# The last pair's stores spread over three queues, later sums of value weights, and a newly planned order, in a linear-attention and gated-unit kernel

## The chip, the cores and the metric

The kernel runs on one core of a Trainium2 chip. Unless said otherwise, times inside an execution are counted from the start of its profiled span, which is about 1.8 us shorter than the device time of the same run. TensorE is "PE" in the profile, its weight loads "PEld", VectorE "DVE", ScalarE "ACT", GpSimd "POOL", SyncE "SP"; a "q" behind a name means that engine's sequencer.

## The reference, cut to what matters

```python
# q, k, v: (8 batches, 8 heads, 576 tokens, 64); everything in float32
kv  = einsum('bhsd,bhse->bhde', k, v)
out = einsum('bhsd,bhde->bhse', q, kv)
x   = out / sqrt(mean(out*out, -1) + 1e-6) * g_norm      # -> (8, 576, 512)
gate = sigmoid(causal convolution of x with 5 taps per channel)
result = ((x @ w_val) * gate) @ w_out                    # w_val, w_out: 512 x 512
```

The two weights reach the kernel as 64-bit floats. They are narrowed to 32 bits on the chip, in eight steps for each quarter of a weight: five on VectorE and three on ScalarE.

## The kernel before

One function holds a small scheduler. Every piece of work is a step with an engine, a planned duration, a wanted start and needs. The scheduler turns the steps into one order per engine, and that order is fixed in the program. A table of shifts, found by a search, moves the wanted starts. Four parts:

```python
    def keep_warm(n):                       # filler: products with the identity
        if n > 0:
            new_kv(0)
        for _ in range(n):
            nc.tensor.matmul(..., ident[:], ident[:], start=True, stop=True)
    ...
    def store(i, c):                        # four rows of blocks, one DMA each
        ot = st["ot", i, c]
        for j in range(HB):
            ...
            nc.sync.dma_start(
                out=rows_out[2 * i + bb, n], in_=ot[j * TB:(j + 1) * TB, :])
    ...
    for n in range(4):                      # sums of value weights, on VectorE
        plan.add(
            "DVE", 0.61, begin + 20.0 + n, val_sums, n, ...
        )
    ...
        idle_from = 9.0
        for start, step in plan.order():
            if step["engine"] == "PE" and start < 60.0:
                keep_warm(int((start - idle_from) / 0.3))
                idle_from = start + step["time"]
            step["fn"](*step["args"])
```

Wherever the plan has TensorE idle in the first 60 us, the program puts one identity product per 0.3 us of planned idleness, which stops the engine from standing still. Each such product shows as two records in the trace.

The batches are worked in pairs. The output of the last pair ends with three groups of four stores each: "block 6", "block 7" and the "single" block of what is left over of both batches.

## Time and profile before

| | before |
|---|---|
| time, median of 3 runs | 337.14 us (337.06 to 337.18) |
| profiled span, granted clock (of another run, of 338.08 us) | 336.3 us, 0.998 |
| first value product starts (timeline of TensorE) | 42.54 us |
| last product ends (timeline of TensorE) | 330.44 us |
| last store issued, last store landed (DMA landings) | 333.25 us, 334.95 us |

The views that carry this are in the prediction below. The chain of waits is read from top to bottom as start, length and who held things up. In the table by stretches each engine has its busy time with the number of instructions behind it.

### The profile page before, as it was taken

The numbers are of one execution on the slowest core, as the hardware profiler recorded it, in microseconds if no ns is written. First come the engines' busy times: TensorE is split into PE (matmuls) and PEld (weight loads), VectorE is DVE, ScalarE is ACT, GpSimd is POOL, SyncE is SP. The second block draws the span as 40 slices with busy tenths as digits, with TensorE's granted clock in tenths as the row PEclk, the third lists the DMA queues.
The fourth block names the chain that finished last, engine by engine and source line by source line (L and its number), as shares of the span: only waits on it lengthen the run. The fifth ranks groups of instructions, "written<-read, shape, count | busy, mean of one in ns | idle before, by whom it ended". The sixth has DMA issues, their size and how long they took to land.

```text
span 336.3 us, 6403 instructions
## 1 busy us (share of the span) xinstructions
PE 319.1 (95%) x2251; PEld 256.2 (76%) x2251; DVE 281.8 (84%) x504; ACT 151.7 (45%) x325; POOL 140.4 (42%) x178
## 2 busy tenths in 40 slices
PE   2978999999999999999999999999999999999992
PEld 2978878888888878857878877688888577888761
DVE  4535979999999999999788799999989999989601
ACT  5357686585234464352445325343446143534220
POOL 3004603733677438926604478532962193000000
PEclk9999999999999999999999999999999999999999
DMA  6999995699699597577944699622520035220232
GB/s 199 268 305 357 283 248 178 160 251 294 188 232 236 123 259 212 138 209 188 302 111 132 166 258 244 156 55 67 133 63 0 17 87 117 57 55 16 62 95 64
DMA packets 46014, 55.38 MB, mean 165 GB/s; under 512 B 15754, under 2 KB 36254, under 8 KB 45982
## 3 DMA queue, kind: packets, MB, share of 16 engines
q1 hardware_dynamic: 42750, 48.67, 53.9%
q0 software_dynamic: 3072, 6.30, 8.1%
q8 instruction: 18, 0.29, 0.4%
q14 instruction: 14, 0.11, 0.1%
q10 hardware_dynamic: 160, 0.00, 0.0%
HBM read 39.21 MB, written 9.44 MB: 145 GB/s over the span
## 4 chain that ended last, share of the span: by engine, by line
PE 85%; DVE 5%; SPq 4%; DMA 2%; issue 1%; ACT 1%; DVEq 0%; ACTq 0%
PE val L582 19%; PE a L720 14%; PE cb L720 12%; PE raw L484 10%; PE va L632 9%; PE kv L407 6%; PE vc L632 4%; PE out L663 4%; PE vb L632 2%; DMA k<-in_k_dram 2%; PE xTps L530 2%; SPq L267 2%; DVE gate L570 2%; PE qTps L445 1%; SPq L290 1%
## 5 line engine op out<-in xcount | busy, mean ns | idle before, releaser
L512 POOL TENSOR_TENSOR rt<-ss,mhalf 128x8 f32<-128x8 f32 (+1 forms) x40 | 71.0, 1785 | 100.4 <-DVE ss L506 100.3
L570 DVE SCALAR_TENSOR_TENSOR gate<-xT,cwT,gate 128x576 f32<-128x576 f32 x128 | 98.8, 810 | 1.6 <-ACT gate L564 1.3
L553 POOL DMA_DIRECT2D xT<-y x96 | 52.8, 557 | 35.9 <-PE a L720 14.3
L582 PE MATMUL val<-xT,wval 128*128 128x288 f32 x256 | 65.7, 408 | 0.0
L582 PEld LDWEIGHTS val<-xT,wval 128*128 128x128 f32 x256 | 47.6, 190 | 12.9 <-ACT xT L537 0.8
L484 PEld LDWEIGHTS raw<-kvbd,qT 128*128 128x128 f32 (+1 forms) x320 | 35.4, 180 | 6.0 <-issue 2.6
L484 PE MATMUL raw<-kvbd,qT 128*128 128x128 f32 (+1 forms) x320 | 38.9, 280 | 0.8 <-DVE x L520 0.8
L498 ACT ACTIVATE sq<-raw 128x512 f32<-128x512 f32 (+1 forms) x40 | 22.1, 553 | 26.6 <-PE raw L484 26.5
L720 PE MATMUL a<-wsum,sums 128*128 128x256 f32 x128 | 33.5, 384 | 0.6 <-ACT ot L731 0.6
L506 DVE TENSOR_REDUCE ss<-sq 128x8 f32<-128x520 f32 (+1 forms) x40 | 25.3, 633 | 9.7 <-ACT sq L498 9.5
L577 ACT ACTIVATE gate<-gate 128x576 f32<-128x576 f32 x32 | 21.7, 684 | 12.5 <-DVE gate L570 12.3
L720 PEld LDWEIGHTS a<-wsum,sums 128*128 128x128 f32 x128 | 23.7, 190 | 4.7 <-ACT ot L731 1.0
L595 DVE TENSOR_TENSOR gv<-gv,gate 128x576 f32<-128x576 f32 x32 | 23.6, 750 | 2.8 <-ACT gate L577 1.6
L591 ACT COPY gv<-val 128x288 f32<-128x288 f32 x32 | 12.7, 396 | 28.9 <-PE val L582 28.7
L520 DVE TENSOR_TENSOR x<-raw,rt 128x512 f32<-128x512 f32 (+1 forms) x40 | 24.7, 622 | 0.3 <-PE xTps L530 0.3
L729 DVE TENSOR_TENSOR ot<-cb,ot 128x256 f32<-128x256 f32 x32 | 13.4, 420 | 13.7 <-ACT ot L733 9.5
L564 ACT ACTIVATE gate<-xT,cwT 128x576 f32<-128x576 f32 x32 | 23.6, 773 | 1.0 <-DVE gv L595 0.8
L407 PEld LDWEIGHTS kv<-v,k 128*64 128x64 f32 x512 | 17.6, 137 | 6.7 <-issue 5.5
L407 PE MATMUL kv<-v,k 128*64 128x64 f32 x512 | 20.7, 226 | 1.8 <-DMA k<-in_k_dram 1.8
L632 PE MATMUL va<-xs,vsum 128*128 128x288 f32 x64 | 18.1, 406 | 0.0
L720 PE MATMUL cb<-wout,sums 128*128 128x256 f32 x64 | 17.2, 390 | 0.6 <-DVE ot L729 0.2
L720 PE MATMUL cb<-wsum,sums 128*128 128x256 f32 x64 | 16.7, 384 | 0.3 <-DVE sums L696 0.3
(106 smaller groups left out, 510.1 us busy)
## 6 DMA issues: line engine op xcount, KB each, us to landing
q<-in_q_dram SPq DMA_DIRECT2D x96, 140.0 KB, 3.9
out_dram<-ot SPq DMA_DIRECT2D x144, 64.0 KB, 1.7
v<-in_v_dram SPq DMA_DIRECT2D x16, 512.0 KB, 7.3
k<-in_k_dram SPq DMA_DIRECT2D x16, 512.0 KB, 7.5
xT<-y POOLq DMA_DIRECT2D x96, 64.0 KB, 3.6
w_wval<-in_moe_w_val_dram SPq DMA_DIRECT2D x4, 512.0 KB, 6.2
q<-in_q_dram SPq DMA_DIRECT2D x4, 512.0 KB, 8.2
w_wout<-in_moe_w_out_dram SPq DMA_DIRECT2D x4, 512.0 KB, 6.4
```

Source lines behind the costliest of these rows:

```text
L407: nc.tensor.matmul(kvp[r * D:(r + 1) * D, hp, :], st["k", b, half][:, h, j, :] if j < NJ else kl[:, 2 * hp + r, :], st["v", b, half][:, h, ...
L484: nc.tensor.matmul(raw[row * m:(row + 1) * m, col * P:(col + 1) * P], st["qT", b][:, hp, c * P:c * P + m], kv_bd[b % 2][:, hp, :], start=T ...
L506: nc.vector.reduce_sum(out=ss[:, 0:n], in_=st["sq", b, c][:, 0:n], axis=AX.X)
L512: nc.gpsimd.tensor_tensor(out=rt[:, 0:n], in0=st["ss", b, c][:, 0:n], in1=mhalf[:, 0:n], op=ALU.pow)
L520: nc.vector.tensor_tensor(out=x[:, 0:n * D].rearrange("p (h e) -> p h e", h=n), in0=st["raw", b, c][:, 0:n * D].rearrange("p (h e) -> p h ...
L553: nc.gpsimd.dma_start(out=xTs[b % 2][i * TB:(i + 1) * TB, :, first:first + P], in_=y[a * TB:(a + 1) * TB, i])
L564: nc.scalar.activation(out=gate[:], in_=xTs[b % 2][:, jt, HALO:SX], func=AF.Copy, scale=cwT[:, K - 1, jt:jt + 1])
L570: nc.vector.scalar_tensor_tensor(out=gate[:], in0=xTs[b % 2][:, jt, tap * TB:tap * TB + S], scalar=cwT[:, tap, jt:jt + 1], in1=gate[:], op ...
L582: nc.tensor.matmul(val[:], wval[:, kc, jt * P:(jt + 1) * P], xTs[b % 2][:, kc, HALO + n * SV:HALO + (n + 1) * SV], start=(kc == 0), stop=( ...
L595: nc.vector.tensor_tensor(out=both, in0=both, in1=st["gate", b, jt][:], op=ALU.mult)
L632: nc.tensor.matmul(st[bank, "val", b, mj][:], weights_[:, k], tokens()[:, k], start=(n in (0, 1, 3) and k == 0), stop=(k == NK // 2 - 1), ...
L720: nc.tensor.matmul(st[bank, i, p], tokens()[:, k], weights_[:, k], start=(n < 2 and k == 0), stop=(k == NK // 2 - 1), skip_group_check=True)
```

## The change

Intent: GpSimd and ScalarE take some of the last pair's stores, so that fewer issues stand one behind the other on SyncE. The sums of value weights (four VectorE operations) are wanted at 150 us of the plan; so far they were wanted soon after the first batch and ran at 40.2 to 42.8 us. Planned durations are corrected to measured ones, and the order is searched anew, so the whole table of shifts is different. The diff, cut to its core:

```diff
 SHIFTS = {
     ... (every entry is different)
-    def store(i, c):
+    def store(i, c, cols=slice(0, C), queues=(nc.sync,)):
         ot = st["ot", i, c]
         for j in range(HB):
             ...
-            nc.sync.dma_start(
-                out=rows_out[2 * i + bb, n], in_=ot[j * TB:(j + 1) * TB, :])
+            queues[j % len(queues)].dma_start(
+                out=rows_out[2 * i + bb, n, :, cols], in_=ot[j * TB:(j + 1) * TB, cols])
...
-                "PE", 0.87 * part, t, raw_product, b, c,
+                "PE", 0.905 * (1.0 if c < NJ else 0.62), t, raw_product, b, c,
...  (four more durations: 1.75 -> 1.82, 1.93 -> 1.95, 3.45 -> 3.6, 0.885 -> 0.9)
+                if b == B - 1 and m:
+                    last_stores(chunk, r, t + 6.8)
+                    continue
...
+    def last_stores(chunk, r, want):
+        kept = lambda n: ("kept", (chunk[0], 3, n))
+        if r == 0:                                   # block 6
+            plan.add("POOL", 2.4, want, store, *chunk, slice(0, C), (nc.gpsimd,), ...)
+            return
+        plan.add("SP", 2.0, want, store, *chunk, HIGH, (nc.sync,), ...)       # block 7
+        plan.add("SP", 1.0, want + 1.0, store, *chunk, LOW, (nc.sync, nc.scalar), ...)
...
-            "DVE", 0.61, begin + 20.0 + n, val_sums, n,
+            "DVE", 0.61, 150.0 + n, val_sums, n,
```

More of the change, by code (lines that the diff above doesn't have):

```diff
@@ L21 @@
 SHIFTS = {
-    "fast_product": {0: -31.5, 1: 1.5, 2: -4},
-    "gate_tap": {0: 13, 1: 77, 2: 43, 3: 77, 4: 87, 5: 70.5, 6: 69.5, 7: 67.5},
-    "keep_x": {0: -25},
-    "kv_product": {5: -4.5, 6: -4.5, 7: -10.5},
-    "load_half": {("k", 0): 7.5, ("k", 1): 13.5, ("k", 3): 6.5, ("k", 4): -7, ("k", 5): 34.5,
-        ("k", 6): 3.5, ("v", 0): -60.5, ("v", 1): 19.5, ("v", 2): 27.5, ("v", 4): 13, ("v", 5): -9.5,
-        ("v", 6): 3, ("v", 7): 9.5},
-    "load_q": {4: -11.5, 5: -12, 6: -14.5, 7: -11.5},
@@ L30 @@
-    "load_tails": {4: 4.5, 5: -101.5, 6: -108.5},
-    "narrow_weight": {("wout", 0): 36, ("wout", 1): 20.5, ("wout", 3): -39},
-    "normalise": {7: 10.5},
-    "out_product": {1: 38.5, 3: -6},
-    "raw_product": {4: -84, 5: -23, 6: -17.5},
-    "square": {2: -9},
-    "stage_weight": {("cw", 0): -235.5, ("wout", 0): 13, ("wout", 1): 22, ("wout", 3): -4,
-        ("wval", 2): -117, ("wval", 3): -123.5},
-    "store": {0: 57.5},
-    "sums": {2: 9.5, 5: -91},
-    "token_sums": {0: 11.5},
-    "turn_blocks": {6: 23, 7: 9},
@@ L42 @@
-    "turn_q": {2: 5.5, 3: 27.5},
-    "turn_x": {1: 3, 3: 7.5},
-    "val_fast": {7: 12.5},
-    "val_product": {0: 33.5, 1: 23, 3: 8.5},
-    "weight_sums": {0: 35.5},
-    "x_sums": {6: -9},
+    "fast_keep": {0: -30, 2: -143.5, 3: -149},
+    "fast_product": {0: -8, 1: 3, 2: 4, 3: -10.5},
+    "gate_start": {1: 5, 7: 29.5},
+    "gate_tap": {1: 42, 2: 73.5, 3: 65, 4: 50.5, 5: 49, 6: 85.5, 7: 69},
+    "gated": {0: 12},
+    "halo": {3: -38.5},
+    "keep_x": {1: 45.5},
+    "kv_product": {2: 28.5, 5: 51.5, 6: 5},
@@ new lines @@
+    "load_half": {("k", 1): 9.5, ("k", 3): -4.5, ("k", 4): -4.5, ("k", 5): 2.5, ("k", 6): -22.5,
+        ("v", 1): 4.5, ("v", 2): -3, ("v", 3): -5, ("v", 4): -5, ("v", 5): -12.5, ("v", 6): -12,
+        ("v", 7): 6.5},
+    "load_q": {7: -19.5},
+    "load_tails": {0: 3.5, 3: -1.5, 4: -19, 5: -19, 6: 16, 7: 7},
+    "narrow_weight": {("wout", 3): -7},
+    "normalise": {2: 15, 6: -146, 7: -9.5},
+    "out_product": {1: -4},
+    "raw_product": {3: -10, 4: -5.5, 5: -15.5, 6: -8.5, 7: 15},
+    "stage_weight": {("cw", 0): -103.5, ("wout", 0): -23, ("wout", 1): 57.5, ("wout", 2): 42.5,
+        ("wval", 1): -83.5, ("wval", 2): -103.5, ("wval", 3): -102.5},
@@ L48 @@
+    "sums": {3: 14.5},
+    "token_sums": {0: -128.5, 2: -20},
+    "turn_x": {7: -9},
+    "val_fast": {7: 2},
+    "val_keep": {5: -41},
+    "val_product": {0: 42.5, 1: 43.5, 2: 2},
+    "x_sums": {5: 14.5, 6: 16.5},
 }
@@ L822, in attention @@
             plan.add(
-                "POOL", 1.75 * part, t + 2.3, powers, b, c, needs=[("ss", key)], gives=[("rt", key)],
+                "POOL", 1.82 * part, t + 2.3, powers, b, c, needs=[("ss", key)], gives=[("rt", key)],
                 takes=[("rt", key)], frees=[("ss", key)],
@@ L853, in attention @@
                     gives=[("xT", b, a), ("moved", b, n)], frees=[("y", b)] if a == 0 else [],
-                    load=0.26 / RATE,
+                    load=0.32 / RATE,
                 )
@@ L937, in products @@
                 plan.add(
-                    "PE", 1.93, t, val_product, b, jt, n,
+                    "PE", 1.95, t, val_product, b, jt, n,
                     needs=[("xT", b, c) for c in HALVES[n]] + [("wval", jt)] + [("val", k) for k in made],
@@ L962, in single @@
         plan.add(
-            "PE", 3.45, first, out_product, *key,
+            "PE", 3.6, first, out_product, *key,
             needs=gated_all(b - 1, b) + [("wout", jt) for jt in range(NK)],
@@ L994, in outputs @@
                 plan.add(
-                    "PE", 0.885, t + 0.88 * n, fast_product, *key,
+                    "PE", 0.9, t + 0.88 * n, fast_product, *key,
                     needs=used + ([("fast", last)] if last else [])
@@ L1023, in outputs @@
             single(b, first + 12.4)
+    def last_stores(chunk, r, want):
+        kept = lambda n: ("kept", (chunk[0], 3, n))
+        if r == 0:
+            plan.add(
+                "POOL", 2.4, want, store, *chunk, slice(0, C), (nc.gpsimd,), needs=[kept(3), kept(5)],
+                frees=[("ot", chunk)], load=0.26 / RATE,
+            )
+            return
+        plan.add(
+            "SP", 2.0, want, store, *chunk, HIGH, (nc.sync,), needs=[kept(4)], frees=[("ot", chunk)],
+            load=0.13 / RATE,
+        )
+        plan.add(
+            "SP", 1.0, want + 1.0, store, *chunk, LOW, (nc.sync, nc.scalar), needs=[kept(6)],
+            frees=[("ot", chunk)], load=0.13 / RATE,
+        )
     def loads_kv(b, want):
```

## The prediction

> **What bounds the kernel now.** I read the page first (busy shares and the 40 slices), then the busy time by stretches, then the waits of TensorE, then the chain that ended last at its two ends, and last the instructions in order of time around the end.
>
> ```profile
> span 336.3 us, 6403 instructions
> PE 319.1 (95%) x2251; PEld 256.2 (76%) x2251; DVE 281.8 (84%) x504; ACT 151.7 (45%) x325; POOL 140.4 (42%) x178
> ...
> PE   2978999999999999999999999999999999999992
> ...
> DVE  4535979999999999999788799999989999989601
> ```
> TensorE is busy nearly without a break from the fifth slice to the last but one, and VectorE is close behind it. The losses that the page shows lie at the two ends. The next view sums busy time by stretch (length; PE; weight loads; VectorE; ScalarE; GpSimd; clock, DMA share, GB/s).
>
> ```profile
> 0.00:22.80 22.80, 14.80 (x149) 14.05 (x149) 9.20 (x35) 12.18 (x27) 2.68 (x10) 1.00 0.98 254
> 22.80:42.60 19.80, 18.86 (x281) 16.57 (x281) 16.05 (x29) 12.67 (x31) 9.64 (x9) 1.00 1.07 316
> ...
> 330.50:336.30 5.80, 0.00 (x0) 0.00 (x0) 0.00 (x0) 0.35 (x1) 0.00 (x0) 0.89 0.35 90
> ```
> For 22.8 us the DMA engines are full (0.98) and TensorE does little of use: much of its 14.8 us is warm-up products with the identity. The last 5.8 us are stores and shutdown alone. Between them TensorE's waits are small:
>
> ```profile
> PE raw L484 <- DVE x L520: 0.8, 1, 0.8
> PE a L720 <- ACT ot L731: 0.6, 1, 0.6
> PE cb L720 <- DVE sums L696: 0.3, 1, 0.3
> PE cb L720 <- DVE ot L729: 0.2, 1, 0.2
> ```
> That is 1.9 us between 44 and 331 us. More is lost in gaps too short to be called waits: after 42.6 us the useful work at the chain's back-to-back durations is 112 output products x 0.865, 32 value products x 1.94, 56 fast value products x 0.97, 4 single products x 3.58, about 28.8 of raw, 17.0 of kv and 3.5 of transposes, together 276.9 us. It took 330.4 - 42.6 = 287.8, so about 11 us go to hand-overs and waits. The chain at the start:
>
> ```profile
> 10.80 1.55 SPq L267
> ...
> 12.40 1.42 SPq L267
> ...
> 13.94 1.05 SPq L309
> ...
> 15.03 7.67 DMA k<-in_k_dram
> ...
> 22.84 1.39 PE kv L407 x40
> ...
> 26.80 0.94 PE kv L396 x6
> 27.73 4.36 PE raw L484 x40
> ```
> The first k of batch 0 lands at 22.70 because it is queued behind four tail loads (two of them for batch 1) and an output weight. All that follows, raw products, GpSimd's powers, normalisation, first value product at 42.6, hangs on it. At the end:
>
> ```profile
> 329.42 1.03 PE L720 MATMUL a<-wsum,gv 128*128 128x256 f32 x4
> ...
> 330.07 3.60 SPq L749 DMA_DIRECT2D out_dram<-ot  x8
> 330.48 0.37 ACT L743 COPY ot<-a 128x256 f32<-128x256 f32 x1 [2.54 <-PE a L720]
> ```
> Eight store issues follow each other on one queue to 333.67, although the last result is ready at 330.85.
>
> **What the Trainium skill says.** "DMA: Bandwidth & Descriptors", section "Issuing engines are not separate DMA queues": transfers from all issuers share the same engines, and several issuers save only issue time. Here issue time is exactly what is exposed (eight at about 0.45 us each, DMA share 0.35), so it can help. The same page, "Latency and other measured facts", has the first byte at about 0.6 us from the hardware path and about 1 us from GpSimd's software path. The trace agrees in kind: stores have a median of 1.7 us from issue to landing, GpSimd's block moves at best 1.9, each taking 0.55 us to issue. "Perfetto Trace Analysis", "Identifying the Most-Contended Engine", warns that matmul busy time overstates closeness to the limit and weight-load time is better: 76% here, which fits the 11 us of small gaps above.
>
> **The change part by part.** No arithmetic is added or removed; the instruction listing of both programs shows the same products. Three parts matter.
>
> (a) Head. The new load order is conv weight, two value weights, q, both k and v halves, then two tails, and only then a third value weight and batch 1's tails. So before the kv products can start, one output weight (512 KB) and two tails (128 KB each) fewer have to land. In the trace the landings of this stretch follow each other by about 1.0 us for a tail and 1.1 to 1.3 for a weight (landings at 16.1, 17.1, 18.2, 19.1 for tails, 20.3 for the weight). That removes about 3.1 us. The second k, the last that kv needs, landed at about 24.3 (its products start at 24.64), so the last input now lands at about 21.2; adding up the new queue by the same spacings from the front gives 20.1. I take 20.8. The four kv groups then run together: 4 x 0.66 = 2.6, end 23.4 instead of 25.98. That is 2.5 us earlier. Against it: warm-ups between kv and raw grow from 6 to 8 products, 2 x 0.11 = 0.2 us later. From raw on the chain is GpSimd's powers (1.09 + 4 x 1.885 us), which don't change, so the first batch's last normalised block comes about 2.4 us earlier. Value weight 0 is now narrowed after it on VectorE (four operations, 2.55 us), but TensorE has transposes (about 3.0 us) and the second half of batch 1's kv (1.3 us) to do meanwhile, so this should hide. Credit: -2.4 us.
>
> (b) Sums of value weights later. Four VectorE operations of 0.68 us at 40.2 to 42.8 us leave the head; they are first needed near 195 us. 2.7 us of VectorE come free just where the first gates wait for it. On TensorE's path this is worth something only if VectorE is what it would wait for; I count it inside (d).
>
> (c) End. The single 64-row product (3.58 us) moves before the last two output products, so the wait of the last cb product for VectorE's addition (about 0.26 us at 328.45) is covered. Let E be the end of the last product. Store 6 goes to GpSimd: its addition ends at about E - 0.4, four issues at 0.55 end at about E + 1.9, the last lands about 2.0 after its issue starts, E + 3.3. The high half of block 7 leaves during the single product. The block of singles: its copy starts at E - 1.7, ends E - 1.1, four issues end about E + 0.7; two low quarters follow on SP and two on ScalarE, landing near E + 2.8 and E + 2.6. Before, the last landing was 333.25 + 1.7 = 334.95, E + 4.5. So the end is worth 4.5 - 3.3 = 1.2 us, with GpSimd's queue last, plus 0.25.
>
> (d) The new order in the middle. Same work, other order. Of the 11 us of gaps I credit 0.8, with a wide spread.
>
> Sum: -2.4 - 1.2 - 0.25 - 0.8 = -4.7 us. 337.1 - 4.7 = 332.4 us.
>
> **Rivals.**
> 1. VectorE takes the head's gain back. From 43 to 314 us it is busy 251.5 of 271 us, and it wakes TensorE for the last sums (0.3 us). Adding up VectorE's work by instruction up to the first batch's last normalisation gives about 4.2 us less in the new order (output weight 3 and part of a value weight come later), so VectorE starts the middle with more still to do, less the 2.7 us of (b), which only move. To end 4 us earlier it must idle about 4 us less after that point, out of 19.5. For it: VectorE is at nine tenths in almost every slice. Against: summing work up to each hand-over of sums, VectorE was 2.4 us behind TensorE at the tightest one (batch 1's sums) in the old order and is nowhere behind in the new. If true, only half of (a) stays: 334 to 335.
> 2. Middle gaps shrink much more, since the order was searched with longer, corrected durations: 3 to 4 us of the 11. Then 329 to 330. Against: named waits sum to 1.9 us only, the rest is hand-over that any order has.
> 3. GpSimd's software path is slower for stores to DRAM than for the block moves, or its end is waited for last: the end gains nothing, 333.6. Or the issue is quicker and SP is last: 0.5 us better.
> 4. A load that the new order delays (batch 1's tails, output weights) becomes a new wait. DMA share falls to 0.8 after 43 us, so I think it small.
>
> **Range and chances.** Head 1.5 to 3.3, end 0.5 to 2.0, middle from 2 lost to 3 gained; taken together 329.4 to 335.6 should hold it 8 times in 10. 2% faster is 330.4; that needs rival 2, one chance in five. Slower by 2% would need a new stall of over 11 us, which nothing suggests.
>
> **What would show it.** Start of the kv products at 20 to 21.5 instead of 22.84, with raw near 25.3 instead of 27.7, and TensorE's unbroken stretch about 2.4 us earlier, show (a). If the first sums and output products of batch 0 are no earlier than before relative to the work done, and VectorE has no idle left to 163 us, rival 1 holds. The distance from the end of the last product to the end of the span, 5.9 us before, should be about 4.7; the last landing should be GpSimd's. The prediction is wrong if the middle loses or gains over 3 us, most likely through waits for VectorE's sums or for normalised blocks.

## More of the kernel before

The metric is the device time of one execution in microseconds (us), as a median over repeated runs.

One line is not in the prediction, and it should have been looked for. It is from the view of the launch line (the line of the program that opens the tile context; all closing instructions carry it) of the kernel before. Its columns are sequencer and operation, count, least, median and greatest duration in ns, and first and last start:

```profile
L1144 POOLq DRAIN  x3: 34/102/11568, 276.7 to 336.0; - x3
```

GpSimd has three closing drains here. The first begins at 276.7 us and takes 11,568 ns, until 288.3. Nothing waits for it then, so it costs nothing and appears in no view of waits.

## The result, and the profile after

The changed kernel took 342.56 us (median of 4 runs, 342.52 to 343.12) against 337.10 us of the kernel before (median of 4 runs of the same rounds, 336.81 to 337.18). The ratio is 1.0167, with a 95% interval of 1.015 to 1.0185. A ratio is the mean time of one kernel's fast runs over that of the other's fast runs of the same rounds, so it is not quite the ratio of the medians. The kernel became 1.7% slower. That is within 2%, but 10 us above the prediction and outside its range.

The page of the profile after, its span and two rows of its 40 slices:

```profile
span 341.3 us, 6395 instructions
...
PE   2899999999999999999999999999999999999970
...
DVE  4606899899899989997998999899999999899210
```

TensorE is as full as before, but its row ends in 7 and 0 where it ended in 9 and 2. The middle of the span looks the same and the end is longer. Busy times by stretch put a number on it (length; PE; weight loads; VectorE; ScalarE; GpSimd; clock, DMA share, GB/s):

```profile
44.10:330.50 286.40, 284.69 (x1784) 224.84 (x1782) 257.21 (x445) 125.53 (x268) 129.33 (x160) 1.00 0.57 149
330.50:335.50 5.00, 0.00 (x0) 0.00 (x0) 0.00 (x0) 0.36 (x1) 1.83 (x4) 0.70 0.41 118
335.50:341.30 5.80, 0.00 (x0) 0.00 (x0) 0.00 (x0) 0.00 (x0) 0.00 (x0) 0.50 0.00 0
```

In the last 5.8 us no engine works and no byte moves. The granted clock of 0.70 and 0.50 in these last two stretches explains why the mean clock of the whole span fell from 0.998 to 0.987 (5.0 x 0.30 + 5.8 x 0.50 = 4.4 us lost of 341). It sank in stretches in which TensorE had no instruction left (0.00 busy), so it held up no product. The last product ends at 330.45 us, against 330.44 before. The last store lands at 334.00, 0.95 us earlier than before. So the stores did what they were meant to do, and something else keeps the program open. The chain of waits ends like this:

```profile
330.34 1.50 POOL out_dram L749 x3
331.84 0.49 POOLq L1165
```

It breaks off at GpSimd's sequencer, on the launch line. SyncE's waits in the last 14 us (engine and line, who released it: total us, times, longest) show how long something was waited for:

```profile
SPq L1165 <- PEq L1165: 6.8, 2, 6.3
```

The name PEq is inferred from semaphore events; TensorE had been done since 330.45. The view of the launch line finds the true one:

```profile
L1165 POOLq DRAIN  x3: 34/102/8918, 331.7 to 341.1; - x3
```

GpSimd's closing drain starts at 331.66 us, takes 8.92 us and ends at 340.57; 0.8 us of barrier later the span is over. GpSimd's last store issue ended at 332.33, and its last store landed at 334.00. The drain therefore ends 8.24 us after the last issue and 6.57 us after the data are in DRAM. In the kernel before it ended 7.92 us after GpSimd's last block move had been issued (280.36), some 48 us ahead of the end.

The second finding lies in the head. The chain of waits after:

```profile
14.95 0.43 PE kv L396 x3
15.38 3.64 PE qTps L445 x64
19.03 3.77 PE kv L396 x32
22.80 2.50 PE kv L407 x80
...
26.12 1.16 PE kv L396 x8
27.28 4.36 PE raw L484 x40
...
34.97 0.60 ACT xT L537
35.57 0.61 ACT wexp_wval L334
36.17 0.61 ACT wexp_wout L334
36.78 0.61 ACT wexp_wval L336
37.40 0.49 ACT xT L537
```

L396 is the warm-up product, L407 the key and value products. The DMA link that led the chain before (k, landing at 22.70) is gone, and the last input of the key and value products now lands at 21.23. Yet they start at 22.8 as before, because 32 records of warm-up products, 3.77 us, stand in TensorE's queue until then. Further down three narrowings of weights stand ahead of a copy of x that TensorE waits for. The first value product starts at 44.06 us against 42.54. At that point the new order has done 1.31 us of key and value products that the old one does just after, so at equal work the head is 0.2 us later, not 2.4 earlier. From there to the last product it took 286.39 us against 287.90 - 1.31 = 286.59 before: the middle gained 0.2.

The account between the two profiled spans, then: head +0.2, middle -0.2, and from the last product to the end 10.90 us instead of 5.86, +5.0. Only the last of the three is beyond the scatter of single profiles. The other profiles of these two orders have the first value product at 41.60 and 41.72 us (experiments 7 and 4, old order) and at 43.19 to 43.79 us (experiments 1, 2, 3 and 8, new order), and the stretch from there to the last product in the new order is 285.94 to 287.45 us. So +0.2 and -0.2 mean that head and middle gained nothing that can be seen.

### The profile page after: what moved, and what is told of

Its sections match the earlier page's. It is cut to its first block, busy times and chain, and to the rows that moved or that the text cites. A ratio compares the mean times of both kernels' runs of the same rounds, so it can differ in the third digit from the quotient of the medians.

```text
span 341.3 us, 6395 instructions
## 1 busy us (share of the span) xinstructions
PE 319.4 (94%) x2247; PEld 257.0 (75%) x2247; DVE 280.6 (82%) x504; ACT 151.4 (44%) x325; POOL 142.7 (42%) x182
## 4 chain that ended last, share of the span: by engine, by line
PE 74%; DVE 10%; DMA 6%; POOL 3%; ACT 2%; SPq 1%; issue 1%; POOLq 0%; DVEq 0%; ACTq 0%
PE val L582 15%; PE a L720 12%; PE cb L720 10%; PE raw L484 8%; PE va L632 8%; PE kv L407 6%; DVE gate L570 6%; PE vc L632 4%; PE out L663 3%; DMA xT<-y 3%; PE kv L396 3%; PE qTps L445 3%; DMA q<-in_q_dram 2%; PE vb L632 2%; PE xTps L530 1%; DVE ot L729 1%
## 5 line engine op out<-in xcount | busy, mean ns | idle before, releaser
L498 ACT ACTIVATE sq<-raw 128x512 f32<-128x512 f32 (+1 forms) x40 | 22.1, 553 | 27.4 <-PE raw L484 26.9
L506 DVE TENSOR_REDUCE ss<-sq 128x8 f32<-128x520 f32 (+1 forms) x40 | 25.2, 632 | 3.6 <-ACT sq L498 3.2
L749 POOL DMA_DIRECT2D out_dram<-ot x4 | 2.0, 504 | 49.3 <-DVE ot L729 49.3
L407 PEld LDWEIGHTS kv<-v,k 128*64 128x64 f32 x512 | 17.6, 138 | 5.1 <-issue 4.2
L407 PE MATMUL kv<-v,k 128*64 128x64 f32 x512 | 20.8, 226 | 0.0
```

The lines of the kernel that those rows point to most:

```text
L407: nc.tensor.matmul(kvp[r * D:(r + 1) * D, hp, :], st["k", b, half][:, h, j, :] if j < NJ else kl[:, 2 * hp + r, :], st["v", b, half][:, h, ...
L506: nc.vector.reduce_sum(out=ss[:, 0:n], in_=st["sq", b, c][:, 0:n], axis=AX.X)
```

## The experiments

Theory A: GpSimd's closing drain takes a fixed time after its last DMA, about 8 us, and since the change it is waited for at the end. Its rivals here: the drain grows with what GpSimd moved (rival B), or any stores on GpSimd cost, wherever they are (rival C). Theory W: the warm-up products, sized by planned idleness, ate the head's gain. Its rival is the prediction's first, that VectorE bounds the middle and takes back whatever the head gains. "Kernel before" below always means runs of the same rounds. Intervals are of the ratio to it.

**1. Block 6 on SyncE.** The changed kernel, with one step edited:

```diff
-                "POOL", 2.4, want, store, *chunk, slice(0, C), (nc.gpsimd,), ...
+                "SP", 2.0, want, store, *chunk, slice(0, C), (nc.sync,), ...
```

> The changed kernel with one edit: the last pair's first block leaves on SP's queue instead of GpSimd's; order of all compute engines is the same. Theory A (GpSimd's closing drain, which stood 8.9 us in the changed kernel's trace and ended 6.2 us after SP was ready to close, is the whole loss): SP then issues 4 + 4 + 2 stores after each other, the last lands about 4.7 us after the last product, so the time falls by about 4.9 us to 337.6 us, and the span ends about 1.4 us after the last landing. Theory B (the new order itself lost time, the drain is only where the end is seen): stays above 341 us.

Measured: 337.20 us (336.62 to 337.93, 4 runs), ratio 1.000 (0.9979 to 1.0021). All of the loss is gone. GpSimd's drain ran from 277.9 to 287.8 us, beside other work.

**2. GpSimd stores, but earlier.** Block 6 on SyncE as in 1; instead GpSimd stores the four rows of block 4, one step earlier, and nothing after:

```diff
+                if b == B - 1 and not m and r == 0:
+                    plan.add("POOL", 2.4, t + 6.8, store, *chunk, slice(0, C), (nc.gpsimd,), ...)
+                    continue
```

> As the first run, but GpSimd stores an earlier block (the last pair but one, ready about 10 us before the end). Theory A: the drain still follows GpSimd's last transfer by about 8 us but ends near 330.5 us, hidden; time as the run with all on SP, 337.6 us within 0.5. Theory C (any use of GpSimd's queue for stores to DRAM costs some 5 us wherever it stands, for example because its last landing is waited for differently): about 342.5 us.

Measured: 337.86 us (337.03 to 338.82, 4 runs), ratio 1.0015 (0.9988 to 1.0043). The launch line of this kernel:

```profile
L1171 POOLq DRAIN  x3: 34/102/8923, 322.0 to 336.2; - x3
```

The drain took 8.92 us again, until 330.95, 8.25 us after the last GpSimd issue ended (322.70). It was over before anyone waited for it. So stores on GpSimd aren't costly as such: rival C falls. Counted from the last landing (325.86) the drain took 5.1 us here and 6.57 in the changed kernel, so the issue is the better point to count from.

**3. One store instead of four.** Block 6 with only its first row on GpSimd:

```diff
-                "POOL", 2.4, want, store, *chunk, slice(0, C), (nc.gpsimd,), ...
+                "SP", 2.0, want, store, *chunk, slice(0, C), (nc.gpsimd, nc.sync, nc.sync, nc.sync), ...
```

> The changed kernel with only one of the four stores of the first block on GpSimd, three on SP. If the drain lasts a fixed time after GpSimd's last transfer (about 8.2 us after its issue ends): issue ends near 330.9, drain near 339.0, time about 341.0 us. If it lasts in proportion to the transfers (a quarter): hidden behind SP's stores, about 337.5 us.

Measured: 340.87 us (340.58 to 341.63, 4 runs), ratio 1.0111 (1.0095 to 1.0127). The launch line:

```profile
L1165 POOLq DRAIN  x3: 34/102/8542, 329.9 to 339.0; - x3
```

The drain ended 8.0 us after the issue of the one store, against 8.24 after the issue of the last of four. It is fixed to within 0.25 us; rival B falls. What three stores fewer save is mainly the issue time of those three, about 1.5 us.

**4. The old order with the new stores.** The kernel before with the two store edits of the diff and nothing else.

> The kernel before with the new stores alone (old order, old durations). Theory A: the whole loss comes with the stores: 342.5 us within 0.5, TensorE's last product at 330.4 as in both. Theory B (order lost time): under 338 us.

Measured: 342.35 us (342.25 to 343.05, 4 runs), ratio 1.0156 (1.0141 to 1.0171), with the drain again ending 8.24 us after the last issue. With the same stores the changed kernel, in the new order, took 0.2 us more. So the stores alone make the whole loss, and the new order is worth nothing that these runs can show.

**5. Half the warm-up products.** The kernel of experiment 1 with one line edited; the order stays the same:

```diff
-                keep_warm(int((start - idle_from) / 0.3))
+                keep_warm(int((start - idle_from) / 0.3) // 2)
```

> The new order with block 6's stores on SyncE (the first experiment's kernel, 337.2 us), and half as many warm-up products in each idle stretch. Theory W (the warm-up products, not the inputs, set when the first key and value products start): they start about 1.4 us earlier relative to the landing of the last tail load, and the raw products about 1.9 us earlier. If TensorE's own work alone bounds what follows, the last product ends 1.5 to 2 us earlier and the time is about 335.5. If the gain is taken back in the middle by VectorE (the prediction's first rival), or the clock falls for want of warm-up, the last product ends where it did and the time stays at 337.2 within 0.5.

Measured: 335.51 us (334.24 to 337.22, 4 runs), ratio 0.9929 (0.9881 to 0.9977). TensorE's timeline, first of experiment 1 and then of this one:

```profile
18.25 3.84 PE L396 MATMUL kv<-ident 128*128 128x128 f32 x32
22.02 0.69 PE L407 MATMUL kv<-v,k 128*64 128x64 f32 x16
```

```profile
17.97 2.05 PE L396 MATMUL kv<-ident 128*128 128x128 f32 x16
19.95 0.69 PE L407 MATMUL kv<-v,k 128*64 128x64 f32 x16
```

The warm-up products end at 20.0 instead of 22.1, and the key and value products start right behind them, at 19.95. The last load that they need landed at 20.17, just before the first products that read it (20.47), so filler and inputs now end nearly together. The first value product came at 40.93 us instead of 43.36 and the last product ended at 326.90 instead of 329.30: 285.97 us apart, against 285.94. A head that is 2.4 us shorter comes out at the end in full in this pair of profiles. Theory W holds for the filler ahead of the key and value products, and the first rival falls. The medians of the two experiments differ by 1.7 us, but they come from different rounds; by their ratios to the kernel before, it is 0.7%, about 2.4 us.

The granted clock didn't fall (0.996 against 0.995), and yet less filler has a price. The 64 turns of q (L445), first in the changed kernel behind 20 warm-up records and then here behind 10:

```profile
15.31 3.71 PE L445 MATMUL qTps<-ident,q 128*64 128x128 f32 x64
```

```profile
12.84 5.20 PE L445 MATMUL qTps<-ident,q 128*64 128x128 f32 x64
```

The same work took 1.5 us longer while the granted clock read 1.00 in both. It took 5.17 and 5.10 us in experiments 9 and 11, which halve the filler too, so halving the filler gives back part of what it saves.

**6. Less VectorE in the middle.** The kernel of experiment 1 without the last gate tap of batches 1 to 7:

```diff
+        if b >= 1 and tap == 0:
+            return
```

> The new order with block 6's stores on SyncE (337.2 us), and on purpose wrong: one gate tap of each group of batches 1 to 7 is left out, 28 VectorE operations of about 0.81 us, 22.7 us of VectorE in the middle; nothing else changes. If VectorE holds TensorE back in the middle (the prediction's first rival), the last product ends 4 us or more earlier and the time is at most 333. If TensorE's own work and hand-over set the pace, it is under 1 us earlier: 336.2 to 337.3.

Measured: 335.57 us (334.99 to 336.50, 4 runs), ratio 0.9937 (0.9887 to 0.9987), between the two expectations. Its output is wrong, which doesn't matter for the time. The stretch from the first value product to the last product, first of experiment 1 and then of this one:

```profile
43.40:329.30 285.90, 284.44 (x1784) 224.63 (x1782) 257.14 (x445) 125.50 (x267) 129.16 (x159) 1.00 0.56 149
```

```profile
43.30:327.60 284.30, 283.57 (x1786) 224.97 (x1782) 237.65 (x417) 124.63 (x267) 124.32 (x159) 1.00 0.57 150
```

VectorE lost 19.5 us of busy time there and TensorE's stretch became 1.6 us shorter. The seven other profiles in this order (the changed kernel and experiments 1, 2, 3, 5, 8 and 9) took 285.94 to 287.45 us for it, and experiment 1 is among the shortest, so the gain is 1.6 to 3.1 us, under the 4 that the first rival asked for. That is what this much less VectorE work wins back of the roughly 11 us that the prediction counted as gaps. The rest stays. An order that moves VectorE work without removing any has less than that to hope for; this last step is argued, not shown.

**7. The late sums alone.** The kernel before, with only the four sums of value weights moved in its fixed order to just before their first use:

```diff
+        late = [f for f in found if f[1]["fn"] is val_sums]
+        found = [f for f in found if f[1]["fn"] is not val_sums]
+        at = next(n for n, f in enumerate(found) if f[1]["fn"] is x_sums)
+        found[at:at] = late
```

> The old order with the old stores, where only the four sums of value weights are moved from the head to just before their first use. Both theories of the middle expect no change of the end: 337.1 within 0.5, since the sums lay beside TensorE's work. If the 2.7 us of VectorE at 40 to 43 us had been on the path to the first gates, the time falls by up to 2 us, to about 335.

Measured: 338.54 us (338.30 to 340.07, 4 runs) against 337.64, ratio 1.0025 (0.998 to 1.007). No gain, and above the expected 337.1 within 0.5; whether it costs a little can't be told from these runs. In its profile the stretch from the first value product to the last product took 289.25 us, against 287.90 before.

**8. Two hardware queues.** The changed kernel with the last pair's stores on SyncE and ScalarE only:

```diff
-                "POOL", 2.4, want, store, *chunk, slice(0, C), (nc.gpsimd,), ...     # block 6
+                "SP", 2.0, want, store, *chunk, slice(0, C), (nc.sync,), ...
-            "SP", 1.0, want + 1.0, store, *chunk, LOW, (nc.sync, nc.scalar), ...     # block 7, low half
+            "ACT", 1.3, want + 1.0, store, *chunk, LOW, (nc.scalar,), (0, 1, 2), ...
+            "SP", 0.5, want + 2.0, store, *chunk, LOW, (nc.sync,), (3,), ...
-            "SP", 2.0, first + 4.3, store, *key, ...                                 # single block
+            for engine, queue, rows in (("ACT", nc.scalar, (2, 3)), ("SP", nc.sync, (0, 1))): ...
```

> The new order with the last pair's stores spread over the two hardware queues only (SyncE and ScalarE), none on GpSimd. Theory A (GpSimd's closing drain, a fixed 8 us after its last software-path transfer, is the whole loss; the spreading itself is worth what the last landing showed, about 1 us): no drain at the end, last landing about 1 us earlier than with the old stores, 336.0 us within 0.5. If spreading the stores is worth nothing once the drain is gone: 337.2.

Measured: 336.67 us (336.08 to 337.09, 6 runs) against 337.64, ratio 0.9961 (0.9926 to 0.9996). The median lies just above the expected 336.0 within 0.5, and the interval only just excludes no gain. The timeline of the end:

```profile
329.32 3.19 SPq L749 DMA_DIRECT2D out_dram<-ot  x7
...
330.99 1.31 ACTq L749 DMA_DIRECT2D out_dram<-ot  x3
```

The last product of this run ended at 330.55, the last store landed at 333.76, the span closed at 334.84. From product to end that is 4.29 us, against 5.86 before. In this profile the whole gain lies at the end, and the last product comes no earlier than before. The idea of the change was sound, then, with queues whose end nobody has to wait for.

**9. Two hardware queues and half the warm-up products.** The edits of 8 and 5 together.

> The new order, the last pair's stores on the two hardware queues (as in the eighth experiment, 336.7 us) and half the warm-up products (as in the fifth, 1.7 us). If both gains are real and lie at different places they add: 335.0 us within 0.5, the last product ending near 328 and the span 4.3 us after it. If one takes the place of the other, no better than 335.5.

Measured: 334.96 us (333.25 to 336.17, 6 runs) against 337.83, ratio 0.9910 (0.9885 to 0.9936). The profile has both gains at their places: the last product ends at 327.18 us, as early as in experiment 5, and the span closes 4.29 us after it, as in experiment 8. The times are in line with a sum, but they don't prove it, since the interval overlaps that of experiment 5 alone (0.9881 to 0.9977).

**10. And a shorter head by hand.** As 9; no warm-up products ahead of the raw products of batch 0, value weight 1's first narrowing behind ScalarE's copies of the key and value products, and output weight 0 narrowed behind the last copy of x:

```diff
+        step = found.pop(find(narrow_weight, "wval", 1, 1))
+        found.insert(find(kv_copy, 0) + 1, step)
+        wide = [... the steps 1 to 7 of narrow_weight "wout" 0 ...]
+        found[at:at] = wide                          # at: behind keep_x of batch 0, block 0
+            if step["fn"] is raw_product and step["args"][:2] == (0, NJ):
+                idle_from = start
```

> As the ninth, and in the head: no warm-up products between the key and value products and the raw products of batch 0 (0.7 us of TensorE after the wait for ScalarE's copies), the narrowing of value weight 1 put behind those copies on ScalarE (0.6 us), and the narrowing of output weight 0 put behind the last copy of batch 0's turned blocks (0.6 us). Theory: the head's gain goes to the end undiminished, so 1.3 to 1.9 us below the ninth, about 333.5. If GpSimd's powers or VectorE's normalisations set the first value product instead, under 0.7 us below the ninth.

Measured: 334.19 us (333.64 to 335.22, 4 runs), ratio 0.9886 (0.9871 to 0.9901). It is the fastest median, 1.1% below the kernel before, but its interval overlaps that of experiment 9, and the expected 1.3 to 1.9 us between them did not come. The raw products started 1.1 us earlier (23.51 against 24.65 us), yet VectorE's timeline shows where that went:

```profile
25.74 0.69 DVE L341 SCALAR_TENSOR_TENSOR wexp_wval<-w_wval,wexp_wval 128x512 uint32<-128x512 uint32 x1 [3.70 <-ACT wexp_wval L338]
26.35 0.42 DVE L506 TENSOR_REDUCE ss<-sq 128x4 f32<-128x260 f32 x1
```

The first sum of squares (L506) stands behind a narrowing step that waited 3.70 us for ScalarE; in experiment 9 that wait was 2.92 us and the sum started at 26.10. Moving a step later on one engine held up the next engine's queue; GpSimd's powers started at 26.92 us, 0.25 later than in experiment 9, and the first value product at 41.93 instead of 41.24.

**11. Half the warm-up products in the old kernel.** The kernel before with the edit of experiment 5.

> The old kernel with half the warm-up products and nothing else. There the first k of batch 0 (landing at 22.7) sets the key and value products, not the warm-up products, so theory W expects the head to gain only what stands between the raw products and the first value product: under 1 us, 336.3 to 337.2. If warm-up products cost as much in the old head as in the new one, 335.5.

Measured: 336.19 us (335.79 to 336.54, 5 runs) against 337.83, ratio 0.9950 (0.9938 to 0.9962): 1.6 us, where at most 0.8 was expected. Theory W was too narrow. In the old head the start of the key and value products is indeed held by k (landed at 22.20, start at 22.34). But the raw products start 4.07 us after it instead of 4.82, which is warm-ups between the two, and another 0.3 us came off between raw and the first value product; the rest of the 1.5 us at the first value product is k's landing, 0.5 us earlier in this run. Experiment 5 against this one is new order against old with the warm-ups trimmed in both, and the stores nearly alike: 0.9929 (0.9881 to 0.9977) against 0.9950. At equal work the head of experiment 5 is 1.4 us ahead of this one (first value product at 40.93 with 1.31 us more of key and value products done, against 41.00). The earlier inputs may be worth that much once the filler is trimmed, but the times don't separate the two.

**12. A second try at the shorter head.** As 10, but the narrowing of value weight 1 is spread behind the first squares and sums, and output weight 0 is put behind the start of the first gates instead of the last copy of x:

```diff
+        put((kv_copy, 0), ("wval", 1, 1))
+        put((square, 0, 4), ("wval", 1, 2))
+        put((square, 0, 2), ("wval", 1, 3))
+        put((sums, 0, 1), ("wval", 1, 4))
+        put((normalise, 0, 3), ("wval", 1, 5))
+        put((sums, 0, 0), ("wval", 1, 6), ("wval", 1, 7))
+        put((gate_start, 0, 1), *(("wout", 0, n) for n in range(1, 8)))
```

> As the tenth, but the narrowing of value weight 1 no longer stands ahead of ScalarE's first squares and VectorE's first sums of squares, which in the tenth delayed GpSimd's powers to 26.9 us, and output weight 0 is narrowed behind the first gates instead of ahead of them. If the order on ScalarE and VectorE was what took the tenth's gain back, GpSimd's powers start near 25.3 us, the first value product near 40.2 us against 41.2 in the ninth, and the time is 333.5 to 334.2. If not, it stays with the ninth and tenth at 334.2 to 335.0.

Measured: 338.63 us (338.15 to 340.15, 7 runs), ratio 1.0016 (0.9979 to 1.0053): a clear miss, 4 us above experiment 10. The powers did start earlier, at 25.57 us. But VectorE's timeline behind the head reads:

```profile
42.13 0.82 DVE L570 SCALAR_TENSOR_TENSOR gate<-xT,cwT,gate 128x576 f32<-128x576 f32 x1 [3.44 <-ACT gate L564]
45.49 0.69 DVE L341 SCALAR_TENSOR_TENSOR wexp_wout<-w_wout,wexp_wout 128x512 uint32<-128x512 uint32 x1 [2.54 <-ACT wexp_wout L338]
...
47.89 5.91 DVE L570 SCALAR_TENSOR_TENSOR gate<-xT,cwT,gate 128x576 f32<-128x576 f32 x8
```

The eight gate taps that follow each other run from 47.89 us; in experiment 9 the taps start at 40.84. VectorE lost 6 us in two waits for ScalarE, and in TensorE's table of waits the longest one for a normalised block is 3.4 us, where experiment 9 has 0.6. VectorE, then, isn't the bound of the middle, but it has no 6 us to give away at this place. That this is the cause is read from the trace.

## Why the prediction was wrong

**(c), the end: this step failed, and with it the number.** Its count of issues and landings was nearly right. GpSimd's four issues ended at E + 1.9, as it said, its last store landed at E + 3.55 for a predicted E + 3.3, and SyncE's last at E + 3.4 for E + 2.8. The last landing moved by 0.95 of the predicted 1.2 us. The wait ahead of the last cb product was covered as predicted: that product starts at 328.52, where the single product ends. What failed is the sentence "So the end is worth 4.5 - 3.3 = 1.2 us": it took the last landing for the end. The end also waits for GpSimd's closing drain, a term that the sum didn't have: 8.24 us after the last GpSimd issue, so E + 10.1. In place of -1.45 the end gave +5.0. Experiments 1 to 4 show it: without late GpSimd stores the loss is gone, with early ones too, with one store most of it stays, and on the old order it is there in full.

**Rival 3** named the place ("its end is waited for last") but gave it the wrong size. It put 333.6 us, the gain lost and nothing more, because it thought of the path's first byte and issue, as the quoted sections of "DMA: Bandwidth & Descriptors" do. Its other half came in part: an issue took 0.50 to 0.52 us instead of 0.55, but SyncE was not last.

**(a), the head: the mechanism was half right.** The inputs landed earlier, at 21.23 for an estimate of 20.8. The step "The four kv groups then run together ... That is 2.5 us earlier" failed. It took the inputs for the only thing that the products wait for, and counted warm-ups between kv and raw (2 x 0.11) but not the 32 records ahead of kv. TensorE was about 3 us behind its plan there. The plan (the scheduler of the kernel, run on its own) has the last turn of q end at 15.9 us; it ended at 19.03. The first turn was planned for 8.0 us and started at 9.90, behind its load, and 20 warm-up records, put into 3.3 us of planned idleness, took 4.43 us, 0.22 each where later ones take 0.12. The fill of 16 products between q and kv stayed as planned. Measured gain at equal work: -0.2 us, for +2.4 predicted. Experiment 5 gets 2.4 us back by halving the fill. But the old kernel gains from that too (experiment 11), and with the fill halved in both the new head is 1.4 us ahead: what became of the other 1.0 us stays open. (a) also trusted that the narrowing on VectorE would hide; it was ScalarE's part of it that stood in front of TensorE, with 0.4 us of named wait and the rest filled by warm-ups.

**(b), the sums:** 2.7 us of VectorE were freed in the head and brought nothing (experiment 7).

**(d), the middle:** 0.8 us credited, 0.2 measured, which is within the scatter, and the comparison of experiment 4 with the changed kernel has the order as a whole 0.2 us slower. Experiment 6 says why little is to be had: even with 19.5 us of VectorE's work gone, the middle shrinks by 1.6 to 3.1.

**Rival 1** did not happen: in experiment 5 what the head gained reached the end in full. Experiment 12 shows its limit: a stall of 6 us on VectorE does pass through.

Of the 10.2 us between prediction and result, 6.5 are the end (+5.0 for -1.45) and 3.2 the head and middle (0.0 for -3.2). The remaining 0.5 is rounding and the difference between profiled spans and medians.

## What to carry to other kernels

The end of a program is the end of its slowest closing wait, not the last landing; before giving a late transfer to another engine, look in the profile of the kernel as it is for that engine's closing drain, even where it is hidden. Here plain stores near the end belong on SyncE and ScalarE, and GpSimd's last transfer has to be issued at least 9 us before the end (an estimate: 8.24 us of drain and 0.8 of barrier in the changed kernel). Filler that a plan sizes becomes a wait of its own once the inputs come earlier or the engine runs behind the plan, so count it among what a step has to wait for, and check what gets slower when it is trimmed; and when a step is moved by hand, look at what stands behind it in the in-order queues of all the engines that take part in it.

## What the Trainium skill lacked or had wrong

- "DMA: Bandwidth & Descriptors", section "SWDGE vs HWDGE vs iDMA", says that the hardware path has the faster setup, and gives plain transfers to SP and ACT and only casting, accumulating or irregular ones to GpSimd. These runs agree with the advice (336.67 us on two hardware queues, 342.56 with GpSimd's), but the larger reason is lacking there: after its last software-path transfer GpSimd's closing drain ended 8.24 to 8.25 us after the issue of the last of four stores, 8.0 after a single one, and 7.92 after the last block move in the kernel before and in all nine experiments in which that move was GpSimd's last transfer.
- "VectorE: DVE Perf Modes", section "The DRAIN you can't avoid", has the boilerplate DRAINs at about 12 ns, constant, on all five engines. The closing drains here differ from that: GpSimd's long one took 8,542 to 11,582 ns, and in the kernel before the others reach from 7 ns on SyncE to 1,620 ns on TensorE's weight loader. Whether these are the drains that the page means is not shown; they carry a line of the kernel's own file. GpSimd's can be what ends the program.
